# One queue for the first loads: plain columns and all of Wq and Wk ahead of the transposing DMAs

## The chip, the core and the metric

The kernel runs on one core of a Trainium2 chip. The metric is the device time of one execution in microseconds. An interval or a median over several executions is given where there are several; a profile is one execution. In the profile's rows PE is TensorE (PEld its weight loads), DVE is VectorE, ACT is ScalarE, POOL is GpSimd and SP is SyncE, which here only issues DMAs. "L619" is line 619 of the kernel.

## What is computed

The input `x` has 2048 rows and 512 columns (bfloat16). Two branches work on it and a gate mixes them:

```
qkv = x @ wqkv                    # 32 heads of 16; q, k, v: 2048 x 512 each
logits[s, w] = q[s] . k[s - 2w] / 4,  w = 0..7   (masked where s < 2w)
a = softmax(logits) over v[s - 2w], then @ wo
h = layernorm(x);  u = gelu(w1^T h + b1)   # 1792 x 512, mixes the rows of x
b = w2^T u + b2                            # 2048 x 512
g = sigmoid((x * gate_w).sum(-1))
out = g * a + (1 - g) * b
```

## The kernel before, in words

**The scheduler.** The kernel is written as a list of operations with engine, estimated duration, and names of what they read and write. A small planner (`_Sched`) runs through them with these estimates and fixes, for each engine, one static order; then waits on semaphores are set where one engine's operation needs another's. For a DMA the estimate of its end is a due time (`lands`) where the code sets one; the first loads have such due times. Priorities and hand-written chains (`chain([...])` from L943 on) set part of the order, VectorE's almost entirely.

**The stages.** TensorE computes the projections Q, K and V (`f_proj`, L614, matmuls at L619), with the weights' columns as the stationary operand and the transposed input XT as the moving one; ScalarE copies each result from PSUM to SBUF (L627 for Q, L630 for K and V). XT is x transposed: 4 slices of 128 columns (d), each with 2048 positions in 4 blocks of 512. VectorE multiplies Q with shifted K (L690), TensorE sums over the head's lanes in two bursts (qkr, L698), ScalarE copies the logits (L728), and VectorE and ScalarE form the softmax. Meanwhile TensorE runs the token MLP: L812 (w1, after the layer norm of x, whose statistics VectorE takes at L574 and ScalarE applies at L598), the GELU at L833, L862 (w2). VectorE forms attention times V (L797 to L802), TensorE multiplies by wo (L878), VectorE mixes both branches (L899), and SP stores the result.

**The first microseconds.** Block 0 of XT comes by two ways. The columns 0 to 127 are loaded as they lie by a plain DMA (d_xp) into XP and turned by four matmuls with the identity matrix (`f_tr`, L541 to L547, named tr0 and tr1), which write PSUM banks 5 and 6; one copy on ScalarE (ev_tra, L555) and one on VectorE (ev_trb, L557) bring them into XT. Columns 128 to 511 of block 0 come by one transposing DMA (d_xt0, L473). Blocks 1 to 3 come by one transposing DMA each (d_xt1 to d_xt3, L460). Until d_xp is there TensorE runs matmuls on a constant (`f_warm`, L537) whose result nobody reads.

**The first loads.** On SP, in this order: d_xp, d_xt0, Wq rows 256 to 383, Wq rows 384 to 511, Wk rows 0 to 255, Wk rows 256 to 511, d_x0 (rows 0 to 255 of x for VectorE's statistics), d_xt1, d_x2, d_x4, d_xt2, d_xt3, and then the rest. ACT issues the two remaining parts of Wq, rows 0 to 127 and 128 to 255, at its start. From d_x2 on each load on SP waits until the one five places earlier in a list (`init_dmas`, `throttle`) has landed.

**The first block of projections.** The 32 matmuls for block 0 of Q and K run over eight PSUM banks: banks 0 to 3 for Q, 4 to 7 for K. The loop at L635 fixes their order: Q with slice d = 0 on four banks, then d = 1, d = 2 and d = 3; then K with d = 0 and 1, then with d = 2 and 3. Behind them come the projections of block 1, which need d_xt1.

## Time and profile before

Three executions took 167.96, 168.19 and 168.55 us, the median is 168.19. The profiled one is the slowest of them.

| | before |
|---|---|
| time of the profiled execution | 168.55 us |
| its span, first to last instruction | 167.3 us |
| TensorE busy | 163.9 us, 98% |
| VectorE busy | 151.3 us, 90% |
| ScalarE busy | 75.0 us, 45% |
| bytes moved by DMA | 29.64 MB, mean 177 GB/s |
| first matmul of the projections | 5.15 us |
| end of the last matmuls' chain | 161.65 us |

The page gives busy time by engine, the chain of work that ended last, and groups of instructions. In the chain each piece has a start, a length and what ran; "issue" is time for which the profile shows no wait. Matmuls are pipelined, so their pace is read from the distance between starts and not from the length of one. A timeline's row merges neighbours of the same kind: start, length, engine, line, operation, count, and in brackets the idle time ahead of it and what ended that. For a DMA the row on SP or ACT is the issuing alone; the data land later, and the answers of the trace on one line of code give that time apart.

### The profile page before, as it was taken

The numbers are of one execution on the slowest core, as the hardware profiler recorded it, in microseconds if no ns is written. First come the engines' busy times: TensorE is split into PE (matmuls) and PEld (weight loads), VectorE is DVE, ScalarE is ACT, GpSimd is POOL, SyncE is SP. The second block draws the span as 40 slices with busy tenths as digits, with TensorE's granted clock in tenths as the row PEclk, the third lists the DMA queues.
The fourth block names the chain that finished last, engine by engine and source line by source line (L and its number), as shares of the span: only waits on it lengthen the run. The fifth ranks groups of instructions, "written<-read, shape, count | busy, mean of one in ns | idle before, by whom it ended". The sixth has DMA issues, their size and how long they took to land.

```text
span 167.3 us, 2152 instructions
## 1 busy us (share of the span) xinstructions
PE 163.9 (98%) x860; PEld 77.6 (46%) x860; DVE 151.3 (90%) x154; ACT 75.0 (45%) x116; POOL 0.7 (0%) x8
## 2 busy tenths in 40 slices
PE   7999999999999999999999999999999999999994
PEld 2455555554454444444444444444444444444463
DVE  0145999999999999999999999999999999999896
ACT  3077688889899818793113121131231321310100
POOL 1000000000000000000000000000000000000000
DMA  5999999968003837996579936462672580000454
GB/s 130 315 272 262 303 322 291 307 196 246 0 0 97 311 115 187 303 290 153 133 183 343 335 129 143 112 187 68 184 218 83 138 223 0 0 0 0 157 190 159
DMA packets 47625, 29.64 MB, mean 177 GB/s; under 512 B 9856, under 2 KB 46464, under 8 KB 47616
## 3 DMA queue, kind: packets, MB, share of 16 engines
q1 hardware_dynamic: 45504, 24.85, 54.0%
q10 hardware_dynamic: 2112, 4.66, 10.0%
q8 instruction: 7, 0.11, 0.3%
q14 instruction: 2, 0.02, 0.0%
HBM read 21.24 MB, written 2.10 MB: 140 GB/s over the span
## 4 chain that ended last, share of the span: by engine, by line
PE 94%; DVE 3%; DMA 2%; issue 0%
PE ps L812 29%; PE ps L862 29%; PE ps L619 25%; PE ps L878 6%; PE ps L698 4%; DVE arena L899 2%; DMA arena<-in_A_x_dram 2%; PE ps L545 0%; DVE arena L557 0%
## 5 line engine op out<-in xcount | busy, mean ns | idle before, releaser
L812 PE MATMUL ps<-arena 128*128 128x512 bf16 x224 | 48.7, 379 | 0.0
L862 PE MATMUL ps<-arena 128*128 128x512 bf16 x224 | 48.7, 379 | 0.0
L619 PE MATMUL ps<-arena 128*128 128x512 bf16 x192 | 42.3, 382 | 0.1
L690 DVE TENSOR_TENSOR arena<-arena 128x4096 bf16<-128x4096 bf16 (+1 forms) x12 | 35.5, 2996 | 2.3 <-ACT arena L630 1.8
L797 DVE TENSOR_TENSOR arena<-arena 128x8192 bf16<-128x8192 bf16 x8 | 35.0, 4419 | 0.0
L812 PEld LDWEIGHTS ps<-arena 128*128 128x128 bf16 x224 | 21.8, 98 | 26.7 <-ACT arena L728 0.4
L862 PEld LDWEIGHTS ps<-arena 128*128 128x128 bf16 x224 | 21.9, 98 | 26.5
L619 PEld LDWEIGHTS ps<-arena 128*128 128x128 bf16 x192 | 21.6, 114 | 20.8 <-DVE arena L557 0.7
L930 ACT ACTIVATE arena<-ps,arena 128x512 bf16<-128x512 f32 x16 | 12.4, 778 | 39.4 <-PE ps L862 39.4
L800 DVE TENSOR_TENSOR arena<-arena 128x4096 bf16<-128x4096 bf16 (+1 forms) x16 | 27.0, 1752 | 0.0
L630 ACT ACTIVATE arena<-ps 128x512 bf16<-128x512 f32 x32 | 18.5, 596 | 4.5 <-PE ps L619 4.5
L833 ACT ACTIVATE arena<-ps,arena 128x512 bf16<-128x512 f32 x14 | 9.6, 687 | 22.2 <-PE ps L812 17.4
L574 DVE BATCH_NORM_STATS2 arena<-arena 128x6 f32<-128x512 bf16 x16 | 10.0, 680 | 5.6 <-DMA arena<-in_A_x_dram 5.6
L878 PE MATMUL ps<-arena 128*128 128x512 bf16 (+1 forms) x80 | 14.2, 337 | 0.0
L899 DVE SCALAR_TENSOR_TENSOR arena<-ps,arena 128x512 bf16<-128x512 f32 (+1 forms) x20 | 11.5, 638 | 0.9 <-PE ps L878 0.7
L598 ACT ACTIVATE arena<-arena 128x512 bf16<-128x512 bf16 x16 | 12.2, 806 | 0.0
L627 ACT ACTIVATE arena<-ps 128x512 bf16<-128x512 f32 x16 | 9.0, 596 | 5.5 <-PE ps L619 5.4
L878 PEld LDWEIGHTS ps<-arena 128*128 128x128 bf16 x80 | 7.8, 98 | 6.3
L674 DVE SCALAR_TENSOR_TENSOR arena<-arena 128x512 bf16<-128x512 bf16 x16 | 10.1, 685 | 0.0
L744 DVE TENSOR_TENSOR arena<-arena 128x512 bf16<-128x512 bf16 (+4 forms) x11 | 7.3, 667 | 0.6 <-ACT arena L763 0.2
L698 PE MATMUL ps<-arena 128*32 128x512 bf16 x128 | 7.3, 380 | 0.0
L728 ACT ACTIVATE arena<-ps 128x512 bf16<-128x512 f32 x8 | 4.7, 592 | 4.6 <-PE ps L698 4.6
(42 smaller groups left out, 40.5 us busy)
## 6 DMA issues: line engine op xcount, KB each, us to landing
arena<-in_B_w_dram SPq DMA_DIRECT2D x7, 1024.0 KB, 8.3
arena<-in_B_w_dram SPq DMA_DIRECT2D x8, 896.0 KB, 5.1
arena<-arena ACTq DMA_DIRECT2D x32, 128.0 KB, 3.0
arena<-in_A_x_dram SPq DMA_DIRECT2D x4, 512.0 KB, 5.1
out_dram<-arena SPq DMA_DIRECT2D x14, 128.0 KB, 1.7
arena<-in_A_x_dram SPq DMA_DIRECT2D x1, 1536.0 KB, 7.9
arena<-in_A_wqkv_dram SPq DMA_DIRECT2D x2, 256.0 KB, 3.6
arena<-in_A_x_dram SPq DMA_DIRECT2D x2, 256.0 KB, 3.5
```

Source lines behind the costliest of these rows:

```text
L598: A("act", (lambda t_: (lambda e: e.activation(out=X[:, t_, :], in_=X[:, t_, :], func=AF.Identity, scale=col(RSTD, t_), bias=col(NMR, t_)) ...
L619: ins = e.matmul(ps[:, bank, s0:s1], lhsT=lhsT, rhs=XT[:, dt, sb * 512 + s0:sb * 512 + s1], start=(dt == 0 and s0 == 0), stop=(dt == 3))
L630: return lambda e: e.activation(out=dst, in_=ps[:, bank, :], func=AF.Copy)
L690: return lambda e: e.tensor_tensor(out=PBL[buf][:, :, 512 * c0:512 * (c0 + nc_)], in0=in0, in1=in1, op=ALU.mult)
L698: ins = e.matmul(ps[32 * c:32 * c + 32, 4 + wl, :], lhsT=RP, rhs=PBL[buf][:, wl, c * 512:(c + 1) * 512], start=(dl == 0), stop=(dl == 3), ...
L797: A("dve", (lambda o_, i0, i1: (lambda e: e.tensor_tensor(out=o_, in0=i0, in1=i1, op=ALU.mult)))(pv, in0, in1), 4.4, reads=v_res + ["atx_% ...
L800: A("dve", (lambda pv_, n__: (lambda e: e.tensor_tensor(out=pv_[:, 0:n__], in0=pv_[:, 0:n__], in1=pv_[:, n__:2 * n__], op=ALU.add)))(pv, n ...
L812: ins = e.matmul(ps[:, bank, :], lhsT=W1W[:, slot, st, 128 * e_:128 * e_ + 128], rhs=X[:, st, :], start=(st == 0), stop=(st == NST - 1))
L862: ins = e.matmul(ps[:, bank, :], lhsT=W2S[slot][:, ft, 128 * e_:128 * e_ + 128], rhs=UT[:, ft, :], start=(ft == 0), stop=(ft == NFT - 1))
L878: ins = e.matmul(ps[:, bank, 0:c1 - c0], lhsT=OT[:, t, 128 * i:128 * i + 128], rhs=WO[:, t, c0:c1], start=(t == 0), stop=(t == 3))
L899: A("dve", (lambda i_, b_, c0_, c1_: (lambda e: e.scalar_tensor_tensor(out=T1[:, i_, c0_:c1_], in0=ps[:, b_, 0:c1_ - c0_], scalar=col(G, i ...
L930: A("act", (lambda i_, bank_: (lambda e: e.activation(out=T1[:, i_, :], in_=ps[:, bank_, :], func=AF.Identity, scale=col(OMG, i_), bias=co ...
```

## The change

The first loads all go to SP, in a new order, and the transposing DMA of block 0 shrinks to columns 256 to 511; columns 128 to 255 come as a second plain slice and are turned by TensorE like the first.

- SP's order is now: slice 0 of block 0 (d_xp0), Wq rows 0 to 127, Wk rows 0 to 127, slice 1 (d_xp1), then for d = 1, 2, 3 one load each with the 128 rows of both Wq and Wk (d_wqk1 to d_wqk3, 256 KB each), d_xt0 with 256 columns, d_xt1, and only then d_x0 and the rest. ACT issues none of them.
- `turn(dt, prev)` holds the two pairs of turning matmuls and their two copies; it is called for slice 0 ahead of the projections and for slice 1 between Q's and K's products with slice 0.
- The matmuls on a constant are five of 512 columns and one of 256 ahead of the turning (before: six and one), and one of each behind it (before: one of 512).
- The order of the first 32 projections: Q with d = 0, the turning of slice 1, K with d = 0 on the banks 4, 7, 5, 6, then Q and K with d = 1, Q with d = 2, Q with d = 3, and K with d = 2 and 3.
- The due times of the first loads are new, and VectorE's chain has the copy of slice 1 behind that of slice 0.

```diff
         def ld_xt0():
-            dst = XT[:, 1:4, 0:512]
-            op = sch.dma("sp", lambda e: e.dma_start_transpose(dst, x2d[0:512, 128:512]), 512 * 384 * 2, ds, issue=1.25,
-                         writes=XT0[1:4], after=prev_dma(), name="d_xt0")
+            dst = XT[:, 2:4, 0:512]
+            op = sch.dma("sp", lambda e: e.dma_start_transpose(dst, x2d[0:512, 256:512]), 512 * 256 * 2, ds, issue=1.25,
+                         writes=XT0[2:4], after=prev_dma(), name="d_xt0")
...
-        first_loads = [ld_w(0, 0, 1, "act"), ld_xt0(), ld_w(0, 1, 1, "act"), ld_w(0, 2, 1), ld_w(0, 3, 1), ld_w(1, 0, 2), ld_w(1, 2, 2),
-                       ld_x(0, 2)]
+        XP = view("OUTS", BF16, [(512, 2), (128, 4), (1, 128)])
+
+        def ld_xp(dt):
+            op = sch.dma("sp", mk_dma(XP[:, dt], xv[:, 0:4, 128 * dt:128 * dt + 128]), 512 * 128 * 2, sch.dsem("xp%d" % dt),
+                         writes=["outs%d" % dt], after=prev_dma(), issue=0.4, name="d_xp%d" % dt)
...
+        def ld_qk(d):
+            op = sch.dma("sp", mk_dma(WQKV[:, d, 0:2 * D], wqkv_v[:, d, 0:2 * D]), 2 * 128 * D * 2, ds,
+                         writes=["wqkv0_%d" % d, "wqkv1_%d" % d], after=prev_dma(), issue=0.45, name="d_wqk%d" % d)
...
+        first_loads = [ld_xp(0), ld_w(0, 0, 1), ld_w(1, 0, 1), ld_xp(1), ld_qk(1), ld_qk(2), ld_qk(3), ld_xt0()]
         ld_xt(1)
         first_loads.append(init_dmas[-1])
-        for op_, t_ in zip(first_loads, (3.5, 5.7, 5.0, 6.3, 6.7, 7.6, 8.6, 9.4, 11.0)):
+        first_loads.append(ld_x(0, 2))
+        for op_, t_ in zip(first_loads, (3.1, 3.8, 4.3, 4.7, 5.4, 6.1, 6.8, 8.0, 10.0, 10.9)):
             op_.lands = t_
             op_.deps.clear()
-        first_loads[2].order.add(first_loads[0])
-        init_dmas[:] = [first_loads[1]] + first_loads[5:]
+        init_dmas[:] = first_loads[5:]
...
-        A("pe", f_warm(6), 2.56, writes=["lg7_0", "lg7_1"], name="warm1", prio=-100)
+        def turn(dt, prev):
+            for h in range(2):
+                lgr = ["lg%d_0" % (5 + h), "lg%d_1" % (5 + h)]
+                prev = A("pe", f_tr(dt, h), 0.215 if dt == 0 else 0.11, reads=["outs%d" % dt, "ident"], writes=lgr, after=[prev],
+                         name="tr%d%d" % (dt, h), prio=-100 if dt == 0 else 0)
+                dst = XT[:, dt, 256 * h:256 * h + 256]
+                pin = ps[:, 5 + h, 0:256]
+                if h == 0:
+                    A("act", ...activation(out=d_, in_=i_, func=AF.Copy)..., reads=lgr, writes=["xt0_%d" % dt], name="ev_tra%d" % dt, prio=0)
+                else:
+                    A("dve", ...tensor_copy(out=d_, in_=i_)..., reads=lgr, writes=["xt0_%db" % dt], name="ev_trb%d" % dt, prio=0)
+            return prev
+
+        A("pe", f_warm(5), 2.13, writes=["lg7_0", "lg7_1"], name="warm1", prio=-100)
         w2_ = A("pe", f_warm(1, 256), 0.2, writes=["lg7_0", "lg7_1"], name="warm2", prio=-100)
...
+        tr_ = turn(0, w2_)
         A("pe", f_warm(1), 0.43, writes=["lg7_0", "lg7_1"], after=[tr_], name="warm3", prio=-100)
...
+        w3_ = A("pe", f_warm(1, 256), 0.2, writes=["lg7_0", "lg7_1"], after=[tr_], name="warm4", prio=-100)
...
-        for (b0, d0, d1, s0, s1) in ((0, 0, 1, 0, 512), (0, 1, 2, 0, 512), (0, 2, 3, 0, 512), (0, 3, 4, 0, 512), (4, 0, 2, 0, 512), (4, 2, 4, 0, 512)):
-            for b in range(b0, b0 + 4):
+        for (bs, d0, d1, s0, s1) in ((range(4), 0, 1, 0, 512), ((4, 7, 5, 6), 0, 1, 0, 512), (range(8), 1, 2, 0, 512),
+                                     (range(4), 2, 3, 0, 512), (range(4), 3, 4, 0, 512), (range(4, 8), 2, 4, 0, 512)):
+            if bs == (4, 7, 5, 6):
+                last_main[0] = turn(1, last_main[0])
+            for b in bs:
...
-        chain(["rp", "ev_trb"] + ln1(0, 1, 2, 3) + ["qkm_0_0_0", "qkm_0_1_0"] + ln1(4, 5, 6, 7) + ln2(0)
+        chain(["rp", "ev_trb0", "ev_trb1"] + ln1(0, 1, 2, 3) + ["qkm_0_0_0", "qkm_0_1_0"] + ln1(4, 5, 6, 7) + ln2(0)
```

## The prediction

> **What bounds the kernel now.** I read the page first (the busy shares and the chain by engine), then the chain of waits in order of time, then the timeline of each queue over the first 20 us, where the change lies, and last the places further down where TensorE and VectorE hand over to each other.
>
> The page says that TensorE is the chain:
>
> ```profile
> span 167.3 us, 2152 instructions
> ...
> PE 163.9 (98%) x860; PEld 77.6 (46%) x860; DVE 151.3 (90%) x154; ACT 75.0 (45%) x116; POOL 0.7 (0%) x8
> ...
> PE 94%; DVE 3%; DMA 2%; issue 0%
> ```
>
> The chain in order of time (start, length, what) shows where its other 6% are:
>
> ```profile
> 0.80 3.10 DMA arena<-in_A_x_dram
> ...
> 4.04 0.60 PE ps L545 x4
> ...
> 4.66 0.44 DVE arena L557
> ...
> 5.15 33.44 PE ps L619 x152
> ...
> 154.73 6.92 PE ps L878 x32
> 161.65 0.03 issue
> 161.68 3.98 DVE arena L899 x9
> ```
>
> From 5.15 to the end TensorE never waits. Only the first 5.15 us are something else: 3.10 us for the plain slice d_xp, 1.24 us from its landing (3.91) to the first projection. So the change can act in three ways alone: it moves the 5.15, it adds TensorE work, or it opens a gap after 5.15.
>
> The timeline of the weight loads, one ahead of each matmul, shows the pace:
>
> ```profile
> 2.50 0.15 PEld L537 LDWEIGHTS ps<-const-bfloat16-1.0 128*128 128x128 bf16 x1 [0.28 <-issue]
> 2.92 0.15 PEld L537 LDWEIGHTS ps<-const-bfloat16-1.0 128*128 128x128 bf16 x1 [0.28 <-issue]
> ...
> 5.14 0.15 PEld L619 LDWEIGHTS ps<-arena 128*128 128x128 bf16 x2 [0.68 <-DVE arena L557]
> 5.56 0.15 PEld L619 LDWEIGHTS ps<-arena 128*128 128x128 bf16 x1 [0.27 <-issue]
> 5.98 13.99 PEld L619 LDWEIGHTS ps<-arena 128*128 128x128 bf16 x65 [0.28 <-issue]
> ```
>
> Up to 5.98 a 512-column matmul comes every 0.43 us, after it 65 in 13.99 us, 0.215 each. TensorE ran at half pace until about 6.1 us (the granted-clock column reads 1.00 throughout, so I go by the spacing). With three matmuls at the slow pace, the fourth at 6.26 and 28 more at 0.216, the first 32 projections (block 0 of Q and K) end at 12.5.
>
> SP's issues:
>
> ```profile
> 0.80 0.43 SPq L429 DMA_DIRECT2D arena<-in_A_x_dram  x1
> 1.29 1.64 SPq L473 DMA_TRANSPOSE arena<-in_A_x_dram  x1
> ...
> 5.07 0.47 SPq L429 DMA_DIRECT2D arena<-in_A_x_dram  x1
> 5.58 3.25 SPq L460 DMA_TRANSPOSE arena<-in_A_x_dram  x1
> ```
>
> and VectorE's start and its first hand-over with TensorE (L698 is the burst of logits qkr_0, from 38.59 in the chain):
>
> ```profile
> 9.08 1.29 DVE L574 BATCH_NORM_STATS2 arena<-arena 128x6 f32<-128x512 bf16 x2 [3.99 <-DMA arena<-in_A_x_dram]
> 11.95 1.29 DVE L574 BATCH_NORM_STATS2 arena<-arena 128x6 f32<-128x512 bf16 x2 [1.59 <-DMA arena<-in_A_x_dram]
> 15.08 4.49 DVE L690 TENSOR_TENSOR arena<-arena 128x4096 bf16<-128x4096 bf16 x2 [1.84 <-ACT arena L630]
> ...
> 35.08 2.28 DVE L690 TENSOR_TENSOR arena<-arena 128x4096 bf16<-128x4096 bf16 x1
> ...
> 42.20 4.43 DVE L690 TENSOR_TENSOR arena<-arena 128x8192 bf16<-128x8192 bf16 x1 [0.41 <-PE ps L698]
> ```
>
> VectorE idles for DMA until 11.95 and for ScalarE's copy of K until 15.08; its last product for the burst ends at 37.36, 1.2 us before the burst starts, and after it VectorE waits 0.41 for TensorE. So VectorE may come about 1.2 us later before TensorE feels it.
>
> **Part 1: the first slice arrives earlier.** Now d_xp (128 KB) shares its time with Wq's first rows, issued by ACT at 0.80 (2.9 us to landing); after the change nothing is issued beside it, and the next DMA follows on the same queue. How long it takes alone no row shows. Upper end: 3.10, as now. Lower end: 1.7, the page's 128 KB stores. The two 128 KB loads side by side (3.10 and 2.9) are the nearest rows; the change's own due time says 3.1 us of clock time (2.3 after issue), and the old due times stand within 0.4 us of the landings for most of the first loads (3.9 against 3.91 for d_xp, 11.0 against 11.04 for d_xt1). I take half of the 0.8 us: landing at 3.5. One warm-up matmul fewer (0.43) is then idle time anyway. With the same 1.24 us behind it the first projection starts at 4.74 instead of 5.15. Wq's rows, issued at about 1.3, land by 4.2 to 4.4 at 2.9 to 3.1 us each, in time.
>
> The Trainium skill, "DMA: Bandwidth & Descriptors" (Anatomy of one DMA), gives a DMA about 2.0 us fixed plus its bytes at 436 GB/s (fitted for DMAs issued by GpSimd). An estimate by it: 2.3 us for 128 KB, landing at 3.1, and the sum below would be about 0.0 instead of +0.15. The trace does not agree as it stands, with 3.10 us for the same slice beside another load.
>
> But 0.41 us gained before 6.1 us are gained at half pace: at most 0.2 us of full-pace work. The Trainium skill, "TensorE: Matmul & The Clock Gate" (Part 1), says that the clock doubles after a busy window of about 3.4 us which runs freely, by time and not by work; by that rule the doubling stays near 6.1 however early the projections begin. The spacing agrees with a doubling (0.43 to 0.215); what sets its moment this one trace cannot show.
>
> **Part 2: the second slice is turned by TensorE.** Four more 128-column matmuls (tr10, tr11) now lie between Q's and K's first products, on the path. Row: the four of L545 start 0.106 apart at half pace, 0.43 in all; half of that, 0.21, is the lower end. As each needs its own weight load (0.11 for L619), I take 0.36. Their copies (0.38 on ACT, 0.42 on DVE) run while K's banks 4 and 7 are filled (2 x 0.216 = 0.43); K's banks 5 and 6 wait for them. That cover is about as long as the copies: 0.05 us of wait, up to 0.4 without it. Both engines idle there (ACT until 8.62, DVE until 9.08), so nobody else waits.
>
> **Part 3: the sum for TensorE.** Q's first four start at 4.74, 5.17, 5.59 and 6.02, and end near 6.27; turns to 6.63; K's first four with 0.05 wait to 7.54; 24 more at 0.216 to 12.72. Before it was 12.5 (5.98 + 0.28 + 29 x 0.216 = 12.52). So +0.15 to +0.2. With a landing at 3.1 the same sum gives about 12.5 (0.0), with 3.91 about 12.9 (+0.4).
>
> **Part 4: SP's queue and the cover of the loads.** Seven plain issues of 0.43 to 0.56 us plus 0.05 now stand ahead of d_xt0, which starts at about 4.3 instead of 1.29, and takes some 1.1 us (1.64 x 2/3); d_xt1 follows at 5.4 (now 5.58) and d_x0 behind it at about 8.7 instead of 5.07. Later loads of SP move by under 0.4 us. POOL's queue carries no load and is untouched; ACT loses two issues (1.02 us) while it idles, gain nothing.
> When does d_xt0 land? Up to and with it 4 x 128 + 3 x 256 + 256 = 1536 KB are moved; the first eight loads of before are also 1536 KB, and the last of them, issued at 4.55, took 3.8 us: 8.4. TensorE now wants it after 16 instead of 4 products, at 12.72 - 16 x 0.216 = 9.26. Cover 0.9 us; any lateness beyond it is paid in full. d_xt1, 512 KB and some 2 us later (10.4), is wanted at 12.7.
> d_x0 comes 3.6 us later and lands near 11.7, d_x2 near 12.6; VectorE's four statistics (2.6 us) end near 13.9 and it has to be free at 15.08: hidden by its idle time. Without that cover each us goes against the 1.2 us before the burst.
> ACT copies Q's and K's eight block-0 results later and closer together (from about 10.4, 0.48 apart, to 14.2 instead of 13.5), so the copy that VectorE waits for at 15.08 may slip by 0 to 0.3, again within the 1.2. The planner, fed with other due times, may place the bursts one step of 0.86 earlier or later in TensorE's order; without a gap that leaves TensorE's total as it is.
>
> **Sum.** The profiled execution took 168.55 (span 167.3 and 1.25 around it), 0.36 above the median of the three, 168.19. +0.15 makes 168.7 on it, or 168.35 against the median. Its own range, from 0.0 to +0.4 and the spread of the runs shown (167.96 to 168.55): 167.9 to 168.9. A measurement of this kernel tells about 0.3% (0.5 us) from no change.
>
> **Rivals.**
> *Faster: the clock has doubled before the projections start.* Then nothing is gained at half pace. Landing 3.1, first projection 4.3 instead of 5.15, minus 0.21 for the turns at full pace and 0.05 for the copies: -0.6, 167.6. For it: the three runs differ by 0.6 us, as they would if the doubling came now at 6.1 and now before 5.15 (2.35 matmuls x 0.215 = 0.5 us). Against: it needs the early landing as well. By the free-running window that the Trainium skill, "TensorE: Matmul & The Clock Gate" (Part 1), states, such executions would occur by chance. 15%.
> *Slower: d_xt0 lands after TensorE wants it.* Transposing DMAs took 4.2 to 5.8 us from issue to landing; 4.3 plus 5.5 is 9.8, a gap of 0.55 in a chain without slack: +0.7, 168.9, and every us more costs one. It decides from 9.26 on, and reaches 0.3% from about 9.6. Against: those DMAs had plain loads queued ahead, and the count by bytes gives 8.4. 20%.
> *Slower through VectorE:* its statistics end after 16.2, or a burst is placed a step too early: TensorE waits up to 0.9 us, 169.2. Against: 1.2 us of spare. 6%.
> *The change does not do what it says:* d_xp still lands at 3.9, since its 512 short rows and not the neighbour set its 3.10 us. Then only the added turns are left: +0.4, 168.6, within 0.3%. 14%.
> The forecast itself: 45%.
>
> **How the numbers follow.** Within 0.3%: 45 + 14 = 59, a point of which the spread puts elsewhere: 0.58. Faster: 0.15. Slower: 20 + 6 and that point, 0.27. The range, 167.5 to 169.1, takes in the faster rival's 167.6 and the slower ones up to 169.1; about 1 in 10 lies beyond it on each side. The predicted time is the forecast's 168.35.
>
> **What would show it.** Right: d_xp lands before 3.9; the first L619 starts at 4.3 to 5.1; four L545 matmuls more, some 6 us in; no PE wait on a DMA after them; the 33rd L619 matmul at 12.4 to 13.0; VectorE's first L690 still near 15.1. Wrong: a wait of PE for a DMA between 6 and 10 us, the half pace lasting beyond 7 us, or a wait of PE for VectorE at L698.

## The result and the profile after

The changed kernel takes 168.89 us (median; 168.14 to 169.55) against 168.34 us for the kernel before, measured beside it: a ratio of 1.0028, with a 95% interval from 1.0017 to 1.004. It is slower by about half a microsecond; the interval excludes no change, but the ratio lies within the 0.3% that was taken as the bound of "no difference" (the interval reaches beyond it). The profiled execution took 169.34, 0.45 above the median (before's 168.55 stood 0.21 above), so the account below, 0.8 us, is of an execution that lost more than the median one.

The page of the kernel after, its span, busy times and the chain by engine:

```profile
span 168.1 us, 2148 instructions
...
PE 162.8 (97%) x850; PEld 77.7 (46%) x864; DVE 151.6 (90%) x155; ACT 75.1 (45%) x117; POOL 0.7 (0%) x8
...
PE 90%; DMA 3%; DVE 2%; SPq 2%; issue 1%
```

TensorE had 94% of the chain before and has 90% now; SP's issues have appeared in it. The chain in order of time (start, length, what) says where:

```profile
0.80 0.45 SPq L429
...
3.81 0.43 SPq L429
...
4.28 5.46 DMA arena<-in_A_x_dram
9.74 0.14 issue
9.87 3.84 PE ps L638 x17
...
39.39 3.57 PE ps L720 x64
```

The first 9.74 us of the chain are now SP issuing seven plain loads one after the other and then the transposing DMA of the last two slices, d_xt0, 5.46 us from issue to landing. Before, the chain left the DMAs at 3.91. The first burst of logits (L720, before L698) starts 0.80 later than before, at 39.39 instead of 38.59; the last matmul ends 0.81 later (165.94 against 165.13), the span is 0.8 longer. So the whole difference of the two profiles arises before 13.4 us, where block 0 ends.

TensorE's matmuls there (start, length, engine, line, operation, tiles, count, the idle time before them and what ended it; L554 turns slices, L638 projects):

```profile
4.44 1.05 PE L638 MATMUL ps<-arena 128*128 128x512 bf16 x4
5.33 0.39 PE L554 MATMUL ps<-arena 128*128 128x128 bf16 x4
5.56 1.15 PE L638 MATMUL ps<-arena 128*128 128x512 bf16 x4
7.37 1.92 PE L638 MATMUL ps<-arena 128*128 128x512 bf16 x8 [0.67 <-DMA arena<-in_A_wqkv_dram]
9.87 4.48 PE L638 MATMUL ps<-arena 128*128 128x512 bf16 x19 [0.58 <-DMA arena<-in_A_x_dram]
```

Three things are to be seen. The projections start at 4.44 instead of 5.15. They run at full pace from the first on: eight in 1.92 us and already four in 1.05, where before the first ones came 0.43 apart until 6. And there are two waits for a DMA that before did not have: one for d_wqk1 (the second rows of Wq and Wk) and one for d_xt0. The lengths in brackets are idle time of the matrix unit, whose last matmul is counted to the end of its pipeline; counted from start to start they cost more. Eight matmuls from 7.37 at 0.216 are issued by 9.10, and the next comes at 9.87: 0.77. The weight loads of the same stretch give the other:

```profile
6.08 0.27 PEld L638 LDWEIGHTS ps<-arena 128*128 128x128 bf16 x2 [0.41 <-ACT arena L566]
7.37 1.44 PEld L638 LDWEIGHTS ps<-arena 128*128 128x128 bf16 x8 [1.02 <-DMA arena<-in_A_wqkv_dram]
```

The last two products of K's first four start at 6.08 (after a wait of about 0.1 for ScalarE's copy of the second slice) and 6.33; the next could start at 6.54 and starts at 7.37: 0.83.

The account of block 0, from the first projection of before to the end (the 33rd projection starts at 12.52 before and at 13.33 after, +0.81): start -0.71; no half pace any more -0.44 (the first three starts of before are 0.41, 0.43 and 0.28 apart, those of after 0.24, 0.22 and 0.22); four turning matmuls +0.22 (5.33 to 5.56); the copies' wait +0.12; d_wqk1 +0.83; d_xt0 +0.77. The sum is +0.79.

SP's issues, and what VectorE does behind them:

```profile
2.79 1.45 SPq L429 DMA_DIRECT2D arena<-in_A_wqkv_dram  x3
4.28 1.30 SPq L473 DMA_TRANSPOSE arena<-in_A_x_dram  x1
5.63 3.94 SPq L460 DMA_TRANSPOSE arena<-in_A_x_dram  x1
9.61 1.61 SPq L429 DMA_DIRECT2D arena<-in_A_x_dram  x3
```

```profile
12.79 2.47 DVE L593 BATCH_NORM_STATS2 arena<-arena 128x6 f32<-128x512 bf16 x4 [6.61 <-DMA arena<-in_A_x_dram]
15.89 4.49 DVE L712 TENSOR_TENSOR arena<-arena 128x4096 bf16<-128x4096 bf16 x2 [0.62 <-ACT arena L649]
...
43.01 4.43 DVE L712 TENSOR_TENSOR arena<-arena 128x8192 bf16<-128x8192 bf16 x1 [0.42 <-PE ps L720]
```

VectorE's statistics end at 15.26 instead of 13.24, but its first product waits for ScalarE's copy of K in any case and moved by the same 0.81 as TensorE (15.08 to 15.89); behind the burst VectorE waits 0.42 for TensorE, as it waited 0.41 before. VectorE is not in it.

When each load landed, from the semaphore events of the two traces (us from the span's start; issue in brackets):

```
             before                     after
slice 1      3.91 (0.80, beside ACT)    3.21 (0.80, alone)
Wq row 1     3.71 (0.80, ACT)           4.05 (1.30)
Wk row 1     7.44 (4.08, with row 2)    4.44 (1.84)
slice 2      5.73 (1.29, in d_xt0)      4.85 (2.31)
Wq/Wk row 2  4.31 / 7.44                7.33 (2.79)  d_wqk1
Wq/Wk row 3  6.11 / 8.39                8.02 (3.33)  d_wqk2
Wq/Wk row 4  6.45 / 8.39                8.69 (3.81)  d_wqk3
slices 3, 4  5.73                       9.74 (4.28)  d_xt0
d_xt1        11.04 (5.58)               11.57 (5.63)
x0, x2, x4   9.05, 11.93, 13.74         12.77, 13.43, 15.78
d_xt2, d_xt3 15.78, 17.73               17.85, 19.84
```

All of Wq's and Wk's block-0 work needs the same 1536 KB in both kernels. Before, the eight loads that carry it had landed by 8.39; after, by 9.74. The question for the experiments is why.

What the 16 DMA engines did from 0 to 12 us, in slices of 0.3 us (the first row is the share of time in which they were busy, in tenths; the second is GB/s). Of after, then of before:

```profile
DMA  0000002697489999746967999994799999997289
GB/s 0 0 0 0 0 0 55 140 292 254 137 186 282 265 272 296 219 102 205 273 191 282 322 329 259 179 155 82 138 288 279 208 279 293 290 289 169 92 294 386
```

```profile
DMA  0000001469999999998999899999999999869978
GB/s 0 0 0 0 0 0 41 91 143 350 313 349 289 253 291 291 316 366 266 345 294 270 212 324 365 365 373 331 243 167 289 288 290 293 122 164 341 338 219 304
```

Before, the engines are full from 2.7 us on at about 300 GB/s. After, there is a hole near 5.1 (102), and from 7.2 to 8.7 they are mostly busy and yet move only 82 to 259: packets of d_xt0 already stand in engines that are through with their plain loads, and move slowly. Of the 1024 packets of 256 bytes that follow those of the slices, some 470 start before the last plain packet ends at 8.38, at 53 ns each on average; the rest take 19 ns each. The small packets that count the completion of d_wqk3 run between about 6.5 and 8.4, by engine, and those of d_xt0 all at 8.99 to 9.04. So d_xt0 begins while plain loads are still under way, but ends on all engines together, after the slowest of them is done.

### The profile page after: what moved, and what is told of

Read it like the earlier page. It is cut to its first block, busy times and chain, and to the rows that moved or that the text cites. A ratio compares the mean times of both kernels' runs of the same rounds, so it can differ in the third digit from the quotient of the medians.

```text
span 168.1 us, 2148 instructions
## 1 busy us (share of the span) xinstructions
PE 162.8 (97%) x850; PEld 77.7 (46%) x864; DVE 151.6 (90%) x155; ACT 75.1 (45%) x117; POOL 0.7 (0%) x8
## 4 chain that ended last, share of the span: by engine, by line
PE 90%; DMA 3%; DVE 2%; SPq 2%; issue 1%
PE ps L884 29%; PE ps L834 29%; PE ps L638 23%; PE ps L900 6%; PE ps L720 4%; DMA arena<-in_A_x_dram 3%; DVE arena L921 2%; SPq L429 2%
## 5 line engine op out<-in xcount | busy, mean ns | idle before, releaser
L638 PE MATMUL ps<-arena 128*128 128x512 bf16 x188 | 42.1, 379 | 1.6 <-DMA arena<-in_A_wqkv_dram 0.7
L638 PEld LDWEIGHTS ps<-arena 128*128 128x128 bf16 x192 | 21.4, 113 | 22.0 <-issue 1.0
L649 ACT ACTIVATE arena<-ps 128x512 bf16<-128x512 f32 x32 | 18.8, 599 | 3.5 <-PE ps L638 3.3
L646 ACT ACTIVATE arena<-ps 128x512 bf16<-128x512 f32 x16 | 9.3, 602 | 6.7 <-PE ps L638 6.7
L720 PE MATMUL ps<-arena 128*32 128x512 bf16 x128 | 7.3, 380 | 0.0
L750 ACT ACTIVATE arena<-ps 128x512 bf16<-128x512 f32 x8 | 4.7, 592 | 4.6 <-PE ps L720 4.6
```

The costliest lines, as they stand in the source:

```text
L638: ins = e.matmul(ps[:, bank, s0:s1], lhsT=lhsT, rhs=XT[:, dt, sb * 512 + s0:sb * 512 + s1], start=(dt == 0 and s0 == 0), stop=(dt == 3))
L649: return lambda e: e.activation(out=dst, in_=ps[:, bank, :], func=AF.Copy)
L720: ins = e.matmul(ps[32 * c:32 * c + 32, 4 + wl, :], lhsT=RP, rhs=PBL[buf][:, wl, c * 512:(c + 1) * 512], start=(dl == 0), stop=(dl == 3), ...
```

## Experiments

Line numbers in the fences are those of each kernel. All ratios are against the kernel before, measured beside the experiment.

**1. Rows of 1 KB instead of 2 KB.** The suspicion: the joint loads of Wq and Wk have rows of 2 KB where before had 1 KB.

```
-first_loads = [..., ld_xp(1), ld_qk(1), ld_qk(2), ld_qk(3), ld_xt0()]
+first_loads = [..., ld_xp(1), ld_w(0, 1, 2), ld_w(1, 1, 2), ld_qk(3), ld_xt0()]
```

> The changed kernel with two of the three joint loads replaced: Wq rows 128 to 383 and Wk rows 128 to 383 as one load each (rows of 1 KB in SBUF, 256 KB each) in place of the joint loads of Wq and Wk for d = 1 and d = 2 (rows of 2 KB); number of issues, bytes and the order of everything else stay. Theory A (in the changed kernel's profile the joint loads lag on some DMA engines: they take 4.5 to 4.9 us to land, and they hold d_xt0 back): the loads of 1 KB rows take about 3.5 us as before, d_xt0 lands near 8.7 instead of 9.74, TensorE's two waits for DMA (0.67 and 0.58 us) shrink to under 0.4 in sum: 168.89 falls to about 168.2. Theory B (not the rows but the place of the transposing DMA, issued only at 4.28 behind seven plain ones, makes it late): d_xt0 lands at 9.5 to 9.9 as in the changed kernel, 168.9.

Measured: 169.12 us, ratio 1.0042 (1.0023 to 1.0062). The two new loads landed 4.25 and 4.34 us after their issue (7.04 and 7.68), d_xt0 at 9.76. d_xt0 is no earlier, so the length of the rows of these two loads is not the cause (the third, d_wqk3, kept its rows of 2 KB).

**2. TensorE doesn't wait for d_xt0.** The DMAs stay as they are in the kernel after.

```
-rhs=XT[:, dt, ...]                                    # block 0, Q and K
+rhs=XT[:, dt - 2 if sb == 0 and dt > 1 and tn < 2 else dt, ...]
```

> The changed kernel, but for block 0 the products of Q and K with slices 2 and 3 read slices 0 and 1 of the transposed input, so that nothing waits for d_xt0 (the block's columns 256 to 511 are left out of Q and K, slices 0 and 1 counted twice); the loads, the number of matmuls and all orders stay. Theory 1 (what the change costs over the forecast is TensorE waiting for d_xt0): the 0.58 us wait goes, TensorE runs through from the first product with slice 1 on, unless the joint loads for d = 2 and 3 (landing 8.0 and 8.7) take its place: 168.89 falls by 0.4 to 0.6 to 168.3 to 168.5. Theory 2 (the four added matmuls and the half pace at the start set the loss, and the wait is only in the profiled execution): 168.9, unchanged.

Measured: 168.54 us, ratio 1.0015 (0.9992 to 1.0037). TensorE's waits for DMAs:

```profile
7.22 13.14 PE L638 MATMUL ps<-arena 128*128 128x512 bf16 x59 [0.23 <-DMA arena<-in_A_wqkv_dram]
20.59 1.68 PE L638 MATMUL ps<-arena 128*128 128x512 bf16 x7 [0.23 <-DMA arena<-in_A_x_dram]
```

With its reader gone d_xt0 (landed at 9.57) costs nothing. The medians suggest that about half of the loss against before is gone (ratios 1.0028 and 1.0015), but the two intervals overlap (1.0017 to 1.004 and 0.9992 to 1.0037), so the times alone do not show it. A new wait shows at 20.6: d_xt3 landed at 20.46, where before it landed at 17.73. The later loads are 2 to 2.7 us late, and they have a cover of about that size; with block 0 ending 0.8 later they don't show in the kernel after.

**3. The three large weight loads on ACT.** The loads were meant to go out behind ScalarE's load of its table, at about 2 us.

```
-op = sch.dma("sp", mk_dma(WQKV[:, d, 0:2 * D], ...)
+op = sch.dma("act", mk_dma(WQKV[:, d, 0:2 * D], ...)      # d = 1, 2, 3
```

> The changed kernel with the three joint loads of Wq and Wk (d = 1, 2, 3) issued by ACT instead of SP, behind its table load (so from about 2.1 us on, with nothing beside d_xp0), so that SP issues d_xt0 behind d_xp1, at about 2.8 instead of 4.28. Due times and TensorE's order stay. Theory B (d_xt0 is late because it stands behind seven issues on one queue): it lands 1 us or more earlier, by 8.7, both waits of TensorE for DMA fall below 0.4 in sum, 168.2 or less. Theory A (the rows of 2 KB lag and hold d_xt0 back whoever issues them): joint loads still take 4.5 us or more, d_xt0 lands after 9.2, 168.7 to 169.0.

Measured: 170.56 us, ratio 1.0129 (1.0105 to 1.0153). The loads went out at 0.87, 1.29 and 1.85, beside d_xp0, which therefore took 3.50 us and landed at 4.30:

```profile
4.44 0.58 PE L559 MATMUL ps<-arena 128*128 128x128 bf16 x4 [1.09 <-DMA arena<-in_A_x_dram]
...
5.58 1.87 PE L643 MATMUL ps<-arena 128*128 128x512 bf16 x4
7.25 0.63 PE L559 MATMUL ps<-arena 128*128 128x128 bf16 x4
```

Four projections take 1.87 us: half pace, which lasted to about 9.1. So this run was lost at the start. What it shows beside that: d_xt0, issued at 2.79 with only four loads of 128 KB ahead of it on SP, landed at 7.92, 0.93 after the last of them, and from the first projection on TensorE waited for no DMA.

**4. The early slice alone.** The kernel before with ACT's two loads of Wq put into SP's line, behind d_xp, and a warm-up that is one matmul shorter.

```
-first_loads = [ld_w(0, 0, 1, "act"), ld_xt0(), ld_w(0, 1, 1, "act"), ...]
+first_loads = [ld_w(0, 0, 1), ld_xt0(), ld_w(0, 1, 1), ...]
```

> The kernel before with one part of the change alone: no load on ACT, Wq rows 0 to 127 issued by SP right behind d_xp and Wq rows 128 to 255 behind d_xt0 (384 columns), and one warm-up matmul fewer. Slice 0 then arrives with nothing beside it. Forecast's part 1: d_xp lands at about 3.2 as in the changed kernel, first projection near 4.45 instead of 5.15; d_xt0 is issued 0.5 later and lands at 6.2, wanted after four products: at full pace that is 5.3 (a wait of 0.9, nothing gained: 168.3), at half pace 6.15 (no wait, 0.2 to 0.3 gained: 168.1). If a neighbour on the other queue is not what holds d_xp back: 3.9, first projection 5.15, 168.3 to 168.6.

Measured: 169.11 us, ratio 1.0049 (1.003 to 1.0068). The slice landed at 3.27 and the first projection started at 4.51, 0.64 earlier; then

```profile
4.51 1.42 PE L619 MATMUL ps<-arena 128*128 128x512 bf16 x4
6.77 7.39 PE L619 MATMUL ps<-arena 128*128 128x512 bf16 x31 [0.84 <-DMA arena<-in_A_wqkv_dram]
```

Wq's second row landed at 6.63 (before 4.31), Wk's rows at 9.62 and 10.51 (7.44 and 8.39). The time is above what either case of the expectation gave. The early slice is paid for by everything behind it, with the transposing DMA in its old place.

**5. The warm-up filled.** In the profiles so far the pace doubled at moments between about 3.9 and 9.1 us, later where TensorE had idled more in its warm-up. This is the kernel before with that idle time (0.27 and 0.09) given to warm-up matmuls.

```
-w2_ = A("pe", f_warm(1, 256), ...)
+w2_ = A("pe", f_warm(1, 512), ...)
+w3_ = A("pe", f_warm(1, 128), ..., after=[w3_], name="warm4")
```

> The kernel before with TensorE's two idle stretches ahead of the first projection (0.27 us before the turning matmuls, 0.09 us before the first projection) filled with warm-up matmuls; no DMA changes. Theory that TensorE's pace doubles the sooner, the less it idled in its warm-up: the doubling comes before 5.2 us instead of at 6.1, all projections run 0.216 apart, block 0 ends near 12.0 instead of 12.5, 167.9 us. Rival, that the moment of the doubling hangs on something else (time, chance): the projections still start 0.42 apart until about 6.1, block 0 ends at 12.5 to 12.6, 168.3 to 168.5 us.

Measured: 168.37 us, ratio 0.9993 (0.9978 to 1.0008): no gain. In the profiled execution the pace had indeed doubled by the first projection,

```profile
4.99 9.36 PE L619 MATMUL ps<-arena 128*128 128x512 bf16 x41 [0.24 <-DVE arena L557]
```

and block 0 ended at 12.25. The idle time was not all filled: 0.09 us ahead of the turning matmuls and 0.24 ahead of the first projection are left, the latter because the filling matmuls ran at full pace already. The median alone decides little, since 12.25 instead of 12.52 would be worth 0.27 us, which the interval does not exclude. Two other profiles settle it. Experiment 8 has the warm-up of the kernel after and idle time of 0.05 us, like after's 0.06, and half pace to about 6.8. Experiment 9 has before's warm-up up to the turning matmuls and idles 0.26 us ahead of them, as before does 0.27, and its pace had doubled by 4.2 instead of 6.1 (its last two turning matmuls start 0.06 apart, before's 0.107). The theory that idle time in the warm-up sets the moment of the doubling falls for idle times this small.

**6. The large weight loads on ACT, really later.** As 3, but the loads wait for TensorE's second warm-up matmul.

```
+w0_ = A("pe", f_warm(2), 0.85, ...)
+first_loads[4].deps = {w0_}            # d_wqk1, on ACT; d_wqk2 and d_wqk3 behind it
```

> The kernel after with the three 256 KB loads of Wq and Wk issued by ACT, from about 1.8 us on (they wait for TensorE's second warm-up matmul), so that d_xp0 stays alone and d_xt0 moves up on SP to about 2.8 us. If the plain loads queued ahead of d_xt0 on SP are what makes it late: d_xp0 still lands at 3.2 and the first projection still starts near 4.45, d_xt0 lands 4.6 to 5.1 us after its issue, at 7.4 to 7.9, d_wqk1 by 6; TensorE has no wait for a DMA after 4.5, block 0 ends near 12.3 and the time is 168.1 to 168.3. If the bytes that the 16 engines have to carry set it, on whatever queue: d_xt0 lands at 9.3 or later, the two waits of TensorE (0.67 and 0.59 us) keep their sum, 168.9.

Measured: 170.77 us, ratio 1.0142 (1.0118 to 1.0165). The slice came at 2.96, but nothing was won with it. ScalarE:

```profile
1.88 1.44 ACTq L429 DMA_DIRECT2D arena<-in_A_wqkv_dram  x3
3.35 1.28 ACT L567 ACT_TABLE_LOAD   x1 [3.35 <-issue]
4.64 0.38 ACT L567 ACTIVATE arena<-ps 128x256 bf16<-128x256 f32 x1
```

Its table is now loaded behind the three issues, so that its copy of the first slice comes at 4.64 and the first projection at 5.17; and ACT's loads got between Wk's first row (5.83 instead of 4.44) and the second slice (7.11 instead of 4.85), which cost only a wait of 0.11 (0.31 from start to start), since TensorE worked at half pace to 8.7. Again the DMAs tell something else: d_xt0 was issued 1.5 us earlier than in the kernel after and landed 1.1 us earlier, at 8.63, between the two theories, and with it the whole 1536 KB.

**7. ACT's loads of the kernel before held back.** The kernel before, with ACT's two loads waiting for the first warm-up matmul; two queues, the slice first. The warm-up is one matmul of 512 columns shorter and filled up to the first projection.

```
+w0_ = A("pe", f_warm(1), 0.43, ...)
+first_loads[0].deps = {w0_}
```

> The kernel before with ACT's two loads of Wq held back until TensorE's first warm-up matmul is done (about 1.3 us), so that d_xp starts alone though both queues are still used; the warm-up is one 512-column matmul shorter and filled to the first projection. If the early slice is worth something as long as the other loads stay on two queues: d_xp lands near 3.3, the first projection starts near 4.5, Wq's rows land by 4.4 and 5.0, d_xt0 near 5.75 as before (TensorE waits 0.3 us or less for it), block 0 ends at 11.8 to 12.1 instead of 12.5, 167.7 to 167.9 us. If ACT's loads, coming later, hold d_xp or themselves back: d_xp at 3.6 or later or Wq's second rows after 5.8, and 168.3 us or more.

Measured: 169.35 us, ratio 1.0068 (1.0043 to 1.0093).

```profile
4.57 1.26 PE L621 MATMUL ps<-arena 128*128 128x512 bf16 x4 [0.27 <-DMA arena<-in_A_wqkv_dram]
6.78 7.53 PE L621 MATMUL ps<-arena 128*128 128x512 bf16 x34 [0.95 <-DMA arena<-in_A_x_dram]
```

The slice landed at 2.94, but Wq's first row at 4.48, its second at 6.24 and d_xt0 at 6.74 (5.73 before). As in 4, what is taken off the first landing is added to the following ones.

**8. d_xt0 ahead of the last two large loads,** on the one line of the kernel after.

```
-first_loads = [..., ld_qk(1), ld_qk(2), ld_qk(3), ld_xt0()]
+first_loads = [..., ld_qk(1), ld_xt0(), ld_qk(2), ld_qk(3)]
```

> The kernel after with d_xt0 ahead of the last two 256 KB loads (d_wqk2, d_wqk3) on SP, all else in the same order. If the loads ahead of the transposing DMA make it late: d_xt0, issued near 3.3, lands near 8.2 (4.5 to 5.2 us), its wait of TensorE (0.59 us) goes, d_wqk2 and d_wqk3 land by 9.3, where they are wanted; the wait for d_wqk1 (0.67 us at 7.4) stays; about 168.4 us. If the place on the queue doesn't matter: d_xt0 lands at 9.3 or later all the same, or the two weight loads take over its wait, 168.9 us or more.

Measured: 169.09 us, ratio 1.0056 (1.0036 to 1.0077).

```profile
4.50 1.89 PE L638 MATMUL ps<-arena 128*128 128x512 bf16 x4
6.19 0.63 PE L554 MATMUL ps<-arena 128*128 128x128 bf16 x4
6.61 7.61 PE L638 MATMUL ps<-arena 128*128 128x512 bf16 x34
```

d_xt0, issued at 3.34, landed at 7.44 instead of 9.74: its place does decide its landing. But d_wqk2 and d_wqk3 then landed at 9.11 and 9.94, and the 1536 KB were no earlier. In this execution no wait shows, since TensorE worked at half pace to about 6.8 and so wanted everything later. At full pace from the start the third rows would be wanted near 8.3 (an estimate: 4.50, 16 matmuls of 0.216, and 0.34 for the turns and their copies as in the kernel after), 0.8 us before they landed; that would be a wait of the size of the one removed, and the median is no better than that of the kernel after.

**9. The first weight rows back on ACT,** d_xt0 last on SP as in the kernel after: the "one line" undone, and the warm-up has its sixth matmul again.

```
-first_loads = [ld_xp(0), ld_w(0, 0, 1), ld_w(1, 0, 1), ...]
+first_loads = [ld_w(0, 0, 1, "act"), ld_w(1, 0, 1, "act"), ld_xp(0), ...]
```

> The kernel after with only the first rows of Wq and Wk back on ACT (issued from 0.8 us on, beside d_xp0, as before's two loads were); all else stays on SP in the same order, and the warm-up has its sixth matmul again. Theory that the single line is what makes the first 1536 KB late: the eighth load (d_xt0) lands by 8.9 instead of 9.6 to 9.8, TensorE's waits for d_wqk1 and d_xt0 shrink to 0.3 us together or less; d_xp0 lands at 3.9 and the first projection starts at 5.15 again; block 0 ends at 12.3 to 12.9 (by the moment of the doubling), 168.2 to 168.6 us. Rival, that the transposing DMA behind six plain loads is what makes it late, on however many queues: d_xt0 lands at 9.3 or later, 5.3 us or more after its issue, TensorE waits for it 0.3 us or more, 168.9 us.

Measured: 169.49 us, ratio 1.0066 (1.0041 to 1.0091). The single line is not the cause by itself:

```profile
7.54 1.92 PE L639 MATMUL ps<-arena 128*128 128x512 bf16 x8 [0.29 <-DMA arena<-in_A_wqkv_dram]
9.94 4.27 PE L639 MATMUL ps<-arena 128*128 128x512 bf16 x18 [0.48 <-DMA arena<-in_A_x_dram]
```

SP issued d_xt0 0.92 us earlier, at 3.36, and it landed at 9.81, 6.45 us later and no earlier than in the kernel after. The three large loads landed at 7.50, 8.10 and 8.77 (7.33, 8.02, 8.69 in the kernel after), though issued 0.92 us earlier.

**10. Both together.** ACT takes the first weight rows (held back as in 7) and d_xt0 goes ahead of the last two large loads.

```
+first_loads = [ld_w(0, 0, 1, "act"), ld_w(1, 0, 1, "act"), ld_xp(0), ld_xp(1), ld_qk(1), ld_xt0(), ld_qk(2), ld_qk(3)]
+first_loads[0].deps = {w0_}            # after the first warm-up matmul
```

> A kernel made from both: Wq's and Wk's first rows on ACT, held back until TensorE's first warm-up matmul is done; SP issues d_xp0, d_xp1, d_wqk1, then d_xt0, then d_wqk2 and d_wqk3. If two queues deliver 1536 KB by 8.9 and the early slice costs nothing beyond that: d_xp0 near 3.0, the first projection near 4.55, d_wqk1 by 6.6, d_xt0 by 7.8, d_wqk3 by 8.9; waits of TensorE below 0.3 us together, block 0 ends at 11.8 to 12.4, 167.7 to 168.2 us. If what the early slice takes from the other loads is given back in full: Wq's or Wk's rows or d_wqk1 land after they are wanted, waits of 0.5 us or more, 168.4 us or more.

Measured: 168.58 us, ratio 1.0015 (0.9997 to 1.0032).

```profile
4.78 1.02 PE L641 MATMUL ps<-arena 128*128 128x512 bf16 x4 [0.37 <-DMA arena<-in_A_wqkv_dram]
5.64 0.39 PE L555 MATMUL ps<-arena 128*128 128x128 bf16 x4
6.05 8.18 PE L641 MATMUL ps<-arena 128*128 128x512 bf16 x36
```

d_xt0 landed at 6.85 and the whole 1536 KB at 8.25; TensorE waits for Wq's first row, which was held back a little too long (4.69), and by the distance of the starts another 0.19 for Wk's first row (6.01), until 6.05. So the waits and the time are those of the second case.

**11. The three large loads as one.** The kernel after with one DMA of 768 KB, so that SP comes to d_xt0 0.94 us earlier with the same bytes ahead of it.

```
-ld_qk(1), ld_qk(2), ld_qk(3), ld_xt0()
+one DMA: WQKV[:, 1:4, 0:2 * D] <- wqkv_v[:, 1:4, 0:2 * D], ld_xt0()
```

> The kernel after with the three 256 KB loads joined into one DMA of 768 KB, so that d_xt0 is issued at about 3.3 instead of 4.28 with the same bytes ahead of it on the same queue (TensorE has to wait for the whole 768 KB; the time says nothing of the change). If the rate at which SP issues sets the landing: d_xt0 lands about 1 us earlier, at 8.5 to 8.8. If the queue's pace through the bytes ahead sets it: 9.3 to 9.8 as with three loads, now 6 us and more after its issue.

Measured: the 768 KB landed at 9.03, 6.23 us after the issue, and d_xt0, issued at 3.34, at 10.02. TensorE waited for the whole:

```profile
9.07 5.16 PE L638 MATMUL ps<-arena 128*128 128x512 bf16 x23 [1.93 <-DMA arena<-in_A_wqkv_dram]
```

So the rate of SP's issues does not set the landing either. The time, 170.40, is that of one execution and says nothing of the change.

**12. The two lines, held back less.** As 10, with ACT's loads behind a warm-up matmul of 128 columns, at 1.14 and 1.60.

```
-w0_ = A("pe", f_warm(1), 0.43, ...)
+w0_ = A("pe", f_warm(1, 128), 0.11, ...)
```

> The kernel of the two lines with ACT's two loads held back less: they wait for a first warm-up matmul of 128 instead of 512 columns, so that they are issued about 0.35 us earlier, near 1.1 and 1.5 us. If Wq's first row landing late (4.69, TensorE waiting 0.37 us) is the only thing that keeps that kernel from gaining: d_xp0 stays at 3.3, Wq's row lands by 4.4, the first projection starts by 4.5, block 0 ends near 11.8 with an early doubling of the pace, 168.0 to 168.3 us. If ACT's loads hold d_xp0 back again when they come earlier, or the other loads come later for it: the first projection at 4.8 or later or waits for d_wqk1 or Wk's row, 168.5 us or more.

Measured: 168.34 us against 168.40 for before, ratio 0.9998 (0.9979 to 1.0017).

```profile
4.40 1.05 PE L641 MATMUL ps<-arena 128*128 128x512 bf16 x4
5.29 0.39 PE L555 MATMUL ps<-arena 128*128 128x128 bf16 x4
5.87 8.42 PE L641 MATMUL ps<-arena 128*128 128x512 bf16 x38 [0.18 <-DMA arena<-in_A_wqkv_dram]
```

Here the slice lands at 3.16 and Wq's first row at 3.61, the first projection starts at 4.40 as in the kernel after, and one wait of 0.18 is left (Wk's first row, 5.82; 0.35 from start to start). In the profiled execution block 0 ended at 11.96, the earliest of all, and yet the median only equals that of before. It is the best form of the change found, and no gain on the kernel before.

**What the landings say together.** When all of the first 1536 KB had landed, one profile each:

```
                                              d_xt0   all 1536 KB
d_xt0 behind all three 256 KB loads, on SP
  one line       after, 1, 2, (joined) 11     9.74 9.76 9.57 10.02   the same
  first rows on ACT                     9     9.81                   9.81
d_xt0 further ahead, one line
  behind one of the three               8     7.44                   9.94
  third on the line                     4     5.78                   10.51
d_xt0 further ahead, loads on ACT too
  before, 5, 7                                5.73 5.76 6.74         8.39 8.95 8.94
  10, 12                                      6.85 7.00              8.25 9.10
three large loads on ACT, d_xt0 last on SP
  3, 6                                        7.92 8.63              7.92 8.63
```

The six profiles with one line lie between 9.57 and 10.51; so does 9, with two queues but the transposing DMA behind the three large loads. Those with two queues and at most one large load ahead of the transposing DMA on its own queue lie between 7.92 and 9.10. That is one profile each, and before and 5, which issue the same DMAs, differ by 0.56 (10 and 12, with almost the same, by 0.85), so the gap between the groups, 9.10 to 9.57, is within the scatter. The times are clearer: with each half of the change's order undone alone the loss stays (ratios 1.0056 and 1.0066 in 8 and 9, by their intervals at least 1.0036; in 9 the slice is late too, at 3.89). With both undone it is smaller or gone (1.0015 and 0.9998 in 10 and 12, by their intervals at most 1.0032).

## Why the prediction was right and wrong

The measured 168.89 lies in the range (167.5 to 169.1), and the ratio lies just within 0.3%, the side that was given most. But the path was not the one forecast. The likeliest case had TensorE without a wait and 168.35; what happened is the slower rival that was given 20%: d_xt0 lands after TensorE wants it. It had a landing of 9.8 and 168.9 us; the trace has 9.74 and the median is 168.89. That the price fits so well is partly luck, as the terms show: in the profiled execution two gains that the forecast had smaller or not at all (0.8 us together) stand against waits of 1.60 us. The prediction's own sign of being wrong, a wait of TensorE for a DMA between 6 and 10 us, appeared twice (until 7.37 and until 9.87).

- *Part 1, the slice earlier: right, and under-sized.* Alone, the slice takes 2.41 us instead of 3.10; it lands at 3.21 (forecast 3.5, bounds 2.5 to 3.9), and in experiments 1, 2, 4, 8 and 11 it took 2.26 to 2.47. Beside two loads of 128 KB it takes 3.09 to 3.14 (before, 5 and 9), beside three of 256 KB 3.50 (3). So the neighbours did set its time, and the rival that it would still land at 3.9 falls. An estimate by the fit of the Trainium skill, "DMA: Bandwidth & Descriptors" (Anatomy of one DMA), made for DMAs issued by GpSimd, is 2.3 us; the trace agrees for a load that starts alone. The first projection came at 4.44 instead of 4.74, by the same 1.23 behind the landing.
- *The half pace until 6.1: wrong as a fixed point.* I kept the doubling at 6.1, where the one profile had it. In the profile of after it had come by 4.4, which alone is worth 0.44 against before's profile. In 8, with the same start, it came at about 6.8, and in 9 and before, with like idle time, by 4.2 and at 6.1: one profile could not fix it. That is what the faster rival asked for; it occurred, and the waits took it all back.
- *Part 2, the turns: right in kind, and over-sized.* 0.22 us instead of 0.36 (at full pace, the lower end), and 0.12 of waiting for ScalarE's copy instead of 0.05.
- *Part 4, the landing of d_xt0: the step that failed.* "The first eight loads of before are also 1536 KB, and the last of them took 3.8 us: 8.4." The count by bytes supposes that the order and the queue of the loads don't matter. Measured were 9.74, and in four more profiles with the transposing DMA behind the large loads 9.57 to 10.02. Two things make the difference. The transposing DMA does not finish before the loads ahead of it on its queue: it landed 0.93 to 1.52 us after the last of them for 256 KB (ten profiles) and 1.56 to 1.82 for 384 KB (three); only in 7 was it 3.8, with two loads of ACT landing in between. And the plain loads ahead were late themselves: 1280 KB landed by 8.69, where the first 1280 KB of before had landed by 7.44; each of the large ones took 4.5 to 4.9 us from its issue, where before's two of 256 KB took 3.4 and 3.8. The nearest rows that I set against it, "transposing DMAs took 4.2 to 5.8 us from issue to landing", were the better guide: 5.46.
- *A wait that was in no rival:* d_wqk1, 0.83 us. I worked out landing and need only for Wq's first rows and the two transposing DMAs, not for the large loads between them. d_wqk1 is wanted after eight products, at 6.54, and landed at 7.33, 4.54 us after its issue. With it the waits sum to 1.60, more than the rival's 0.55.
- *"Later loads of SP move by under 0.4 us": wrong.* d_x0 landed at 12.77 (forecast 11.7), d_x4, d_xt2 and d_xt3 2.0 to 2.1 us later than before, since SP's second transposing issue, begun at 5.63 as against 5.58, took 3.94 us instead of 3.25, and d_x0's issue now stands behind it: d_x4 and d_xt2 were issued 1.25 later, and took longer from issue to landing (d_x4 5.03 us instead of 4.24). It cost nothing here: VectorE's cover was named, and 0.6 of it was left. Experiment 2 shows whom it reaches next, TensorE at d_xt3.
- *VectorE as the bound:* did not happen, as forecast; its first product and the burst moved by 0.8 with TensorE.

The sum, then: the terms that I had (-0.71, -0.44, +0.22, +0.12) come to -0.81, far better than the forecast +0.15, and the late loads add 1.60. Had the loads come in time, this one execution would have gained what the faster rival said; the median would not, as experiment 12 suggests.

Why doesn't removing most of the lateness (experiment 12) gain those 0.8 us over before? Because 0.44 of them was the early doubling of the profiled execution, which before, if it is a matter of chance, has as often. With a doubling at 6.1 in both, the arithmetic of the forecast holds: four products from 4.40 at half pace to 6.1, 0.23 for the turns, 0.12 for the copies and 28 products at 0.216 give 12.5, against 12.52. Time won before the doubling counts half, and the turns cost what is left. That is an argument from the spacings; the equal medians of 12 and before agree with it.

What stays open is why the plain loads themselves slow down. In the kernel after and in 1, 2 and 9 half of the 16 parts in which the trace counts a landing are there, for the first large load, by 5.4 to 6.3 and the last 0.8 to 2.1 us later (7.04 to 7.50). The parts drift apart, presumably because a few DMA engines fall behind, and the transposing DMA ends after the slowest. In 8, 10 and 12, where the transposing DMA follows directly behind d_wqk1, all its parts land within 0.2 us. That does not show that the engines kept together there: the load directly ahead of the transposing DMA lands like that in the others too (in after d_wqk3, 15 of its 16 parts from 8.62 to 8.69), and in 8 the small packets that count d_wqk1's completion still run between 5.01 and 6.04. But d_wqk1, with the same loads ahead of it, landed at 6.45 in 8 and at 7.33 and 7.18 in after and 2. That suggests that the large loads behind it take part in its lateness; no run takes that apart further. Nor was it tried to put the loads on a third queue.

## What to carry to other kernels

Count the landing of a load from the loads ahead of it on its own queue, not from the bytes of another order: here the transposing DMA of 256 KB landed 0.93 to 1.52 us after the slowest part of what stood ahead of it, so it belongs early on its queue and not behind a run of large loads. When a first load is freed of its neighbours, ask what each following load was given in return, and give a due time to every one of them, not to the last alone. And before a gain is put on a start-up stretch, compare several profiles of it: here the pace of TensorE in that stretch differed by execution as much as the change was worth.

## What the runs showed of the hardware

- *The moment at which TensorE's pace doubles differs between executions of the same instructions.* The kernel after and experiments 1, 2, 8 and 11 have the same TensorE program up to the first projection, at most 0.09 us of idle time of the matrix unit in it, and the same first four loads; the first 512-column matmuls 0.216 to 0.24 apart start at 4.4, 4.4, 5.2, 6.9 and 5.6. With one idle stretch of 0.77 and 1.09 us (6 and 3) it was 8.8 and 9.3. The Trainium skill, "TensorE: Matmul & The Clock Gate" (Part 1), has a window of about 3.4 us that runs freely and a transition that varies by 0.5 us either way; it adds that one kernel had 6, 11 or 14 slow matmuls by the window's phase. The five profiles agree with a free-running window: their spread of 2.5 us is wider than 0.5 us either way, and within the window's length.
- *Two queues.* The Trainium skill, "DMA: Bandwidth & Descriptors" (Rules for kernel authors), says that spreading loads over the issuing engines saves issue time only. Experiment 9 against after agrees: issued 0.92 us earlier, landed no earlier. Experiment 10 against 8 (two queues and one, the transposing DMA ahead of the last two large loads in both) does not fit as easily: the last load was issued 0.94 us earlier and landed 1.69 us earlier (8.25 and 9.94). But in 12, with almost the same DMAs as 10, it landed at 9.10, 0.84 earlier, which the earlier issue covers.
- *The last stretch of a transposing DMA* follows its size: it lands 0.93 to 1.1 us after the last load ahead on its queue for 256 KB in eight of ten profiles, 1.56 to 1.82 for 384 KB, and 1.83 for 512 KB (d_xt1 behind d_xt0 in the kernel after).
